# GpSimd clamps exp to [0, 1] by min and max, and VectorE takes over the subtraction, in a fused convolution and ELU network

## The chip, the cores and the metric

The kernel runs on one core of one Trainium2 chip. The metric is the device time of one execution in microseconds (us), as the median of several runs. In the profiles the engines are PE (TensorE; PEld is its weight loads), DVE (VectorE), ACT (ScalarE), POOL (GpSimd) and SP (SyncE, here only an issuer of DMAs; SPq is its queue). "L237" is line 237 of the kernel that was profiled, so a line's number moves a little from one kernel to the next.

## The reference

```python
# x: (8, 4096, 192), weight: (8 heads, 7), w_in: (192, 2048), w_out: (2048, 192), float32
w   = softmax(weight, axis=-1)
out = causal 7-tap convolution of x along the sequence, one filter per head of 24 channels
h   = out.reshape(32768, 192) @ w_in
g   = np.where(h > 0.0, h, 1.0 * (np.exp(np.minimum(h, 0.0)) - 1.0))     # ELU
return g @ w_out
```

The part that matters is ELU on 32768 x 2048 values. Both kernels compute it as max(h, min(exp(h), 1) - 1): for a positive h the right-hand side is 0 and h wins; for a negative h, exp(h) - 1 is at least h and wins.

## The kernel before

The tokens are cut into 32 tiles of 1024. A tile passes 16 "pairs": a pair is 1024 PSUM columns (two halves of 512) of h. Four engines form a line for each pair, each waiting for the one before by semaphores:

1. TensorE: 12 matmuls fill H, one of three PSUM slots.
2. ScalarE: exp of each half into E (4 buffers in SBUF).
3. GpSimd: min with 1 and subtract 1, in place in E, one instruction a half.
4. VectorE: the maximum of E and H into gT, which frees the PSUM slot.

TensorE also does the second matrix product ("ops") of the tile before, and the convolutions of the tile to come.

```python
CONV_AT = (2, 10)     # the steps, of a tile's 16, at which the next tile's two convolutions are issued
# ... (cut)

            # GpSimd
            for n in range(NP):                       # NP = 32 tiles x 16 pairs = 512
                s, i = divmod(n, NQ)
                if i == 8 and s + NXB < NS:
                    load_x(s + NXB)
                for u in range(2):
                    W(s_exp, 2 * n + u + 1)
                    g.tensor_scalar(
                        out=E[:, n % NE, u, :], in0=E[:, n % NE, u, :],
                        scalar1=1.0, scalar2=1.0, op0=ALU.min, op1=ALU.subtract,
                    ).then_inc(s_clp)
# ... (cut)

            # VectorE
            for n in range(NP):
                s, q = divmod(n, NQ)
                W(s_clp, 2 * n + 2)
                if s >= NG3:
                    W(s_mm2, 2 * (s - NG3 + 1))
                v.tensor_tensor(
                    gT[:, s % NG3, 2 * q : 2 * q + 2, :].rearrange("p f t -> p (f t)"),
                    E[:, n % NE, :, :].rearrange("p u t -> p (u t)"),
                    H[:, slot_of_pair[n] % 3, :],
                    ALU.max,
                ).then_inc(s_tt)
# ... (cut)

            # SyncE: once both convolutions of tile s are evacuated to csb, 20 DMAs
            # regroup them into att, which the tile's first H matmul waits for
                    W(s_ce, m + 1)
                    if s >= 2:
                        W(s_h, NQ * (s - 1))
                    for (hb, sl, r0, nr, j, d0) in MOVES:          # 10 moves
                        for r in range(2):
                            sy.dma_start(
                                att[HP * r + d0 : HP * r + d0 + nr, s % 2, j, :, :],
                                csb[SLOT * sl + r0 : SLOT * sl + r0 + nr, s % 2, hb, :, :],
                            ).then_inc(s_att, 16)
```

The 20 "moves" of a tile can start only after its second convolution, which is issued at step 10 of the tile before.

Of the kernel before, what the change touches and what calls it, by code (L numbers as in the profile page):

```python
# [5 lines left out]
ALU = mybir.AluOpType  # L6
# [14 lines left out]
GS = 512  # L21
# [3 lines left out]
NE = 4  # L25
NG3 = 3
# [17 lines left out]
def bass_lightweight_conv__then__act_elu_kernel(  # L44
# [16 lines left out]
    NQ = NF // 2  # L61
# [9 lines left out]
    slot_of_pair, slot_of_conv, prior = {}, {}, []  # L71
# [21 lines left out]
    for n in range(NP + NQ + LAG + NQ):  # L93
        s, i = divmod(n, NQ)
# [10 lines left out]
    with ExitStack() as stack:  # L105
# [16 lines left out]
        E = sbuf("E", [P, NE, 2, GS], FP32)  # L122
        gT = sbuf("gT", [P, NG3, NF, GS], FP16)
# [10 lines left out]
        H = psum("H", [P, 3, 2 * GS])  # L134
# [14 lines left out]
        s_clp = sema("s_clp")  # L149
        s_tt = sema("s_tt")  # L150
# [30 lines left out]
        @block.gpsimd  # L181
        def _gpsimd(g: bass.BassGpSimd):
            W = Waits(g)

            def load_x(s):
                b, t0 = s % NXB, s * SUP
                if s >= NXB:
                    W(s_cv, 2 * (s - NXB) + 2)
                w0 = 0
                if s % SPB == 0:  # L190
                    g.memset(xg[0:6, b, 0, :], 0.0).then_inc(s_z)  # L191
                    g.dma_start(  # L192
                        xg[6:P, b, 0, :], x_flat[t0 : t0 + P - 6, :]
                    ).then_inc(s_x[b], 16)
                    w0 = 1
                src = bass.AP(
                    tensor=x_flat.tensor,
                    offset=(t0 - 6 + CW * w0) * D,
                    ap=[[D, P], [CW * D, 8 - w0], [1, D]],
                )  # L200
                g.dma_start(xg[:, b, w0:8, :], src).then_inc(s_x[b], 16)  # L201
                g.dma_start(  # L202
                    xg[:, b, 8, :], x_flat[t0 + SUP - P : t0 + SUP, :]
                ).then_inc(s_x[b], 16)

            g.memset(shiftm[:], 0.0).then_inc(s_shift)
            load_x(0)
            W(s_shift, 1)
            for d in range(KSIZE):
                g.affine_select(  # L210
                    out=shiftm[:, d, :],
                    in_=shiftm[:, d, :],
                    compare_op=ALU.not_equal,
                    fill=1.0,
                    base=-d,
                    pattern=[[-1, CW]],
                    channel_multiplier=1,
                ).then_inc(s_shift)
            for r in range(2):
                g.dma_start(  # L220
                    w_in[HP * r : HP * (r + 1), :, :],
                    moe_w_in.rearrange("(j p) n -> p j n", p=HP),
                ).then_inc(s_w, 16)
            for r in range(2):
                g.dma_start(  # L225
                    w_out[HP * r : HP * (r + 1), :, :],
                    moe_w_out.rearrange("(f p) d -> p f d", p=HP),
                ).then_inc(s_w, 16)
            for s in range(1, min(NXB, NS)):
                load_x(s)  # L230
# [7 lines that stand above are left out]
                        out=E[:, n % NE, u, :],  # L238
                        in0=E[:, n % NE, u, :],
                        scalar1=1.0,  # L240
                        scalar2=1.0,
                        op0=ALU.min,
                        op1=ALU.subtract,
                    ).then_inc(s_clp)

        @block.scalar
        def _scalar(a):
            W = Waits(a)
            a.memzero(scr[:, 0:1]).then_inc(s_scr)  # L249
            W(s_scr, 1)  # L250
            a.activation(scr[:, 1:2], scr[:, 0:1], ACT.Exp)
            W(s_set, 2)
            a.activation(wex[:], wq2[:], ACT.Exp).then_inc(s_wex)
            n_half = 0

            def evac(n_half):
                W(s_mm2, n_half + 1)
                b = n_half % 2
                W(s_out[b], 32 * (n_half // 2))
                a.activation(  # L260
                    osb[:, b, :, :, :].rearrange("p g k d -> p g (k d)"),
                    ops[:, :, 0 : 2 * D],
                    ACT.Copy,
                ).then_inc(s_oev)

            for item in order:
                if item[0] == "c":
                    m = item[1]
                    s, g = divmod(m, 2)
                    W(s_cv, m + 1)  # L270
                    if s >= 2:
                        W(s_att, 16 * NDMA_ATT * (s - 1))
                    a.activation(  # L273
                        csb[:, s % 2, :, g, :],
                        H[:, slot_of_conv[m] % 3, :].rearrange("p (b t) -> p b t", b=2),
                        ACT.Copy,
                    ).then_inc(s_ce)
                elif item[0] == "h":
                    n = item[1]
                    k = slot_of_pair[n] % 3  # L280
                    W(s_h, n + 1)
                    W(s_tt, n - NE + 1)
                    for u in range(2):
                        a.activation(  # L284
                            E[:, n % NE, u, :], H[:, k, GS * u : GS * (u + 1)], ACT.Exp
                        ).then_inc(s_exp)
                else:
                    _, t, half, r0, r1 = item
                    if r1 == 2 * NF:
                        evac(2 * t + half)  # L290

        @block.vector
        def _vector(v):
            W = Waits(v)
            v.memset(H[:, 0:2, :], 0.0).then_inc(s_hz)  # L295
            W(s_wq, 16)
            v.tensor_reduce(wmx[:], wq[:], AXIS.X, ALU.max).then_inc(s_set)
            W(s_set, 1)
            v.tensor_tensor(
                wq2[:],  # L300
                wq[:],
                wmx[:, :].unsqueeze(2).to_broadcast([P, HEADS, KSIZE]),
                ALU.subtract,
            ).then_inc(s_set)
            W(s_wex, 1)
            v.tensor_reduce(wsum[:], wex[:], AXIS.X, ALU.add).then_inc(s_set)
            W(s_set, 3)
            v.reciprocal(wrs[:], wsum[:]).then_inc(s_set)
            W(s_set, 4)
            v.tensor_tensor(  # L310
                wprb[:],
                wex[:],
                wrs[:, :].unsqueeze(2).to_broadcast([P, HEADS, KSIZE]),
                ALU.mult,
            ).then_inc(s_set)
            v.wait_ge(s_set, 5)
            k = 5
            for d in range(KSIZE):
                W(s_shift, 2 + d)
                sd = shiftm[:, d : d + 1, :].to_broadcast([P, HEADS, CW])  # L320
                wd = wprb[:, :, d : d + 1].to_broadcast([P, HEADS, CW])
                dst = Tm if d == 0 else Ttmp
                v.tensor_tensor(dst[:, :, :], sd, wd, ALU.mult).then_inc(s_set)  # L323
                k += 1
                W(s_set, k)
                if d:
                    v.tensor_tensor(  # L327
                        Tm[:, :, :], Tm[:, :, :], Ttmp[:, :, :], ALU.add
                    ).then_inc(s_set)
                    k += 1  # L330
                    W(s_set, k)
            n_set[0] = k
            for n in range(NP):
                s, q = divmod(n, NQ)
                W(s_clp, 2 * n + 2)
                if s >= NG3:
                    W(s_mm2, 2 * (s - NG3 + 1))
                v.tensor_tensor(  # L338
                    gT[:, s % NG3, 2 * q : 2 * q + 2, :].rearrange("p f t -> p (f t)"),
                    E[:, n % NE, :, :].rearrange("p u t -> p (u t)"),  # L340
                    H[:, slot_of_pair[n] % 3, :],
                    ALU.max,
                ).then_inc(s_tt)

        @block.tensor
        def _tensor(pe):
            W = Waits(pe)

            def wait_slot(k):
                was = prior[k]  # L350
                if was is None:
                    return
                if was[0] == "h":
                    W(s_tt, was[1] + 1)
                else:
                    W(s_ce, was[1] + 1)

            for item in order:
# [45 lines left out]
                else:  # L404
                    _, t, half, r0, r1 = item
                    if r0 == 0:
                        W(s_tt, NQ * (t + 1))
                        W(s_oev, 2 * t + half)
                    for r in range(r0, r1):
                        kb, f = divmod(r, NF)  # L410
# [80 lines left out]
```

## Time and profile before

| | kernel before |
|---|---|
| median time | 2040.86 us (3 runs, 2040.68 to 2042.27) |
| GpSimd busy | 98% of the span |
| chain of waits that ended last | 95% the GpSimd tensor_scalar |
| mean granted TensorE clock | 0.742 of full |

From the profile page of the kernel before. The first line is busy time and share of the span of each engine; the second the granted TensorE clock in 40 slices, in tenths; then the chain that ended last, by engine and by line; then instruction groups: line, engine, operation, output<-input and count, then busy us and mean ns of one, then the idle time of the engine just before them and who ended most of it.

```profile
PE 1057.4 (52%) x25088; PEld 692.6 (34%) x25088; DVE 640.8 (31%) x531; ACT 670.8 (33%) x1156; POOL 1991.8 (98%) x1120
...
PEclk9568777767777766678777677786666787777867
...
POOL 97%; PE 1%; DVE 1%; SPq 1%; DMA 0%; ACT 0%; issue 0%; POOLq 0%
POOL E L237 95%; POOL xg L201 1%; POOL xg L202 1%; SPq L444 1%; PE ops L415 1%; DVE Ttmp L323 0%; DVE Tm L327 0%; POOL xg L192 0%; DMA wq<-in_weight_dram 0%; DMA att<-csb 0%; ACT csb L273 0%; POOLq L105 0%; ACT osb L260 0%; PE H L395 0%; POOL xg L191 0%
...
L237 POOL TENSOR_SCALAR E<-E 128x512 f32<-128x512 f32 x1024 | 1930.5, 1912 | 26.9 <-ACT E L284 26.4
L338 DVE TENSOR_TENSOR gT<-E,H 128x1024 f16<-128x1024 f32 x512 | 625.4, 1221 | 1377.0 <-POOL E L237 1377.0
```

GpSimd is busy for practically the whole span and the chain consists of it. VectorE was idle 1377 us, all of it ended by GpSimd. The other engines have more than 45% of the span to spare.

From the table of waits of the same kernel (us in total, times, longest):

```profile
DVE gT L338 <- POOL E L237: 1377.0, 512, 25.4
...
PE H L395 <- DVE gT L338: 682.7, 407, 2.9
...
PE H L373 <- DVE gT L338: 222.3, 62, 5.4
...
PE H L395 <- DMA att<-csb: 46.6, 14, 17.3
```

TensorE waits for VectorE, which waits for GpSimd; L395 are the matmuls that make h, L373 the convolutions, which need a PSUM slot too. From the chain in order of time, over one tile (start us, us, what):

```profile
1002.02 60.33 POOL E L237 x32
```

Between two DMA issues that GpSimd makes for each tile stand 32 tensor_scalars in a row, 60.33 / 32 = 1.885 us each. A pair takes 2 x 1.885 = 3.77 us. This spacing is a better measure than the group's mean of 1912 ns, in which neighbours overlap a little.

### The profile page before, as it was taken

To read this page: it belongs to the slowest core of one execution; us is meant where nothing else is said; L and a number is where in the kernel's file an instruction comes from. 1 tells how busy PE (TensorE), PEld (TensorE's weight loads), DVE (VectorE), ACT (ScalarE), POOL (GpSimd) and SP (SyncE) were. 2 spreads that over 40 slices of the span, in tenths; PEclk is the share of its full clock that TensorE was granted. 3 is DMA by queue.
4 is the path that set the end of the run, shared out by engine and by line. 5 is a ranking of instruction groups with operands and counts; after the bars stand their busy time and mean duration, and the time that the engine had idled before them with its cause. 6 is when DMAs were issued, how large, how long until landed. Compare 5 with 4: busy or idle time off the path is not lost.

```text
span 2038.9 us, 54519 instructions
## 1 busy us (share of the span) xinstructions
PE 1057.4 (52%) x25088; PEld 692.6 (34%) x25088; DVE 640.8 (31%) x531; ACT 670.8 (33%) x1156; POOL 1991.8 (98%) x1120
## 2 busy tenths in 40 slices
PE   1454544555545556645445555445565554455466
PEld 0132332333323334323333333333333333333344
DVE  3333333333333333333333333333333333333332
ACT  1333333333333333333333333333333333333332
POOL 4999999999999999999999999999999999999996
PEclk9568777767777766678777677786666787777867
DMA  7111022111121210221110221111211102210001
GB/s 104 25 28 31 25 41 41 34 32 32 28 41 33 39 31 22 41 41 33 36 31 25 41 41 34 31 29 32 41 34 37 30 25 41 41 34 27 23 25 33
DMA packets 97717, 71.17 MB, mean 35 GB/s; under 512 B 52048, under 2 KB 84816, under 8 KB 97488
## 3 DMA queue, kind: packets, MB, share of 16 engines
q1 hardware_dynamic: 54928, 50.40, 9.3%
q0 software_dynamic: 42560, 17.29, 7.8%
q8 instruction: 196, 3.21, 0.6%
q14 instruction: 33, 0.27, 0.0%
HBM read 34.59 MB, written 25.17 MB: 29 GB/s over the span
## 4 chain that ended last, share of the span: by engine, by line
POOL 97%; PE 1%; DVE 1%; SPq 1%; DMA 0%; ACT 0%; issue 0%; POOLq 0%
POOL E L237 95%; POOL xg L201 1%; POOL xg L202 1%; SPq L444 1%; PE ops L415 1%; DVE Ttmp L323 0%; DVE Tm L327 0%; POOL xg L192 0%; DMA wq<-in_weight_dram 0%; DMA att<-csb 0%; ACT csb L273 0%; POOLq L105 0%; ACT osb L260 0%; PE H L395 0%; POOL xg L191 0%
## 5 line engine op out<-in xcount | busy, mean ns | idle before, releaser
L237 POOL TENSOR_SCALAR E<-E 128x512 f32<-128x512 f32 x1024 | 1930.5, 1912 | 26.9 <-ACT E L284 26.4
L338 DVE TENSOR_TENSOR gT<-E,H 128x1024 f16<-128x1024 f32 x512 | 625.4, 1221 | 1377.0 <-POOL E L237 1377.0
L395 PE MATMUL H<-att,w_in 64*64 64x512 bf16 x6144 | 556.4, 478 | 729.5 <-DVE gT L338 682.7
L284 ACT ACTIVATE E<-H 128x512 f32<-128x512 f32 x1024 | 555.8, 595 | 1099.4 <-PE H L395 1099.4
L415 PE MATMUL ops<-w_out,gT 64*64 64x192 f16 x16384 | 530.1, 285 | 7.5 <-DVE gT L338 6.1
L415 PEld LDWEIGHTS ops<-w_out,gT 64*64 64x64 f16 x16384 | 476.7, 130 | 138.6 <-issue 77.1
L395 PEld LDWEIGHTS H<-att,w_in 64*64 64x64 bf16 x6144 | 163.1, 123 | 925.5 <-DVE gT L338 753.1
L373 PE MATMUL H<-Tm,xg 128*24 128x122 bf16 (+3 forms) x2560 | 66.3, 284 | 240.4 <-DVE gT L338 222.3
L373 PEld LDWEIGHTS H<-Tm,xg 128*24 128x24 bf16 x2560 | 55.1, 129 | 278.0 <-DVE gT L338 154.2
L273 ACT ACTIVATE csb<-H 128x1024 bf16<-128x1024 f32 x64 | 65.4, 1023 | 234.5 <-PE H L373 234.5
L260 ACT ACTIVATE osb<-ops 128x768 f32<-128x768 f32 x64 | 52.2, 815 | 28.6 <-PE ops L415 28.5
L201 POOL DMA_DIRECT2D xg<-in_x_dram x32 | 31.0, 968 | 0.0
L202 POOL DMA_DIRECT2D xg<-in_x_dram x32 | 18.4, 575 | 0.0
L323 DVE TENSOR_TENSOR Ttmp<-shift,wprb 128x976 bf16<-128x976 bf16 x6 | 7.0, 1175 | 0.2
L192 POOL DMA_DIRECT2D xg<-in_x_dram x8 | 5.0, 626 | 0.0
L327 DVE TENSOR_TENSOR Tm<-Tm,Ttmp 128x976 bf16<-128x976 bf16 x6 | 4.0, 667 | 0.2
L210 POOL TENSOR_SCALAR_AFFINE_SELECT shift<-shift 128x122 bf16<-128x122 bf16 x7 | 2.7, 456 | 0.1
L225 POOL DMA_DIRECT2D w_out<-in_moe_w_out_dram x2 | 2.2, 1102 | 0.0
L295 DVE MEMSET H<- 128x2048 f32 x1 | 1.8, 1765 | 1.3 <-PEq L476 1.3
L191 POOL MEMSET xg<- 6x192 bf16 x8 | 2.0, 247 | 0.0
L249 ACT ACT_TABLE_LOAD x1 | 1.3, 1283 | 0.7 <-PEq L476 0.7
L220 POOL DMA_DIRECT2D w_in<-in_moe_w_in_dram x2 | 1.3, 644 | 0.0
(14 smaller groups left out, 4.5 us busy)
## 6 DMA issues: line engine op xcount, KB each, us to landing
out_dram<-osb SPq DMA_DIRECT2D x128, 192.0 KB, 2.2
att<-csb SPq DMA_DIRECT2D x384, 48.0 KB
xg<-in_x_dram POOLq DMA_DIRECT2D x24, 384.0 KB, 6.4
att<-csb SPq DMA_DIRECT2D x128, 32.0 KB
xg<-in_x_dram POOLq DMA_DIRECT2D x8, 336.0 KB, 5.4
att<-csb SPq DMA_DIRECT2D x128, 16.0 KB
xg<-in_x_dram POOLq DMA_DIRECT2D x32, 48.0 KB, 5.8
w_in<-in_moe_w_in_dram POOLq DMA_DIRECT2D x2, 768.0 KB, 8.1
```

The lines of the kernel that those rows point to most:

```text
L201: g.dma_start(xg[:, b, w0:8, :], src).then_inc(s_x[b], 16)
L202: g.dma_start(xg[:, b, 8, :], x_flat[t0 + SUP - P : t0 + SUP, :]).then_inc(s_x[b], 16)
L237: g.tensor_scalar(out=E[:, n % NE, u, :], in0=E[:, n % NE, u, :], scalar1=1.0, scalar2=1.0, op0=ALU.min, op1=ALU.subtract,).then_inc(s_clp)
L260: a.activation(osb[:, b, :, :, :].rearrange("p g k d -> p g (k d)"), ops[:, :, 0 : 2 * D], ACT.Copy,).then_inc(s_oev)
L273: a.activation(csb[:, s % 2, :, g, :], H[:, slot_of_conv[m] % 3, :].rearrange("p (b t) -> p b t", b=2), ACT.Copy,).then_inc(s_ce)
L284: a.activation(E[:, n % NE, u, :], H[:, k, GS * u : GS * (u + 1)], ACT.Exp).then_inc(s_exp)
L323: v.tensor_tensor(dst[:, :, :], sd, wd, ALU.mult).then_inc(s_set)
L338: v.tensor_tensor(gT[:, s % NG3, 2 * q : 2 * q + 2, :].rearrange("p f t -> p (f t)"), E[:, n % NE, :, :].rearrange("p u t -> p (u t)"), H[ ...
L373: ins = pe.matmul(H[SLOT * q : SLOT * q + CPH, k % 3, GS * hb + o : GS * hb + o + nc_], xg[:, s % NXB, w, CPH * h : CPH * (h + 1)], Tm[:, ...
L395: ins = pe.matmul(H[HP * c : HP * (c + 1), k % 3, GS * r : GS * (r + 1)], w_in[HP * r : HP * (r + 1), j, HP * f : HP * (f + 1)], att[HP * ...
L415: ins = pe.matmul(ops[HP * c : HP * (c + 1), g, D * kb : D * (kb + 1)], gT[HP * g : HP * (g + 1), t % NG3, f, t0 : t0 + HP], w_out[HP * g ...
L444: sy.dma_start(att[HP * r + d0 : HP * r + d0 + nr, s % 2, j, :, :], csb[SLOT * sl + r0 : SLOT * sl + r0 + nr, s % 2, hb, :, :],).then_inc( ...
```

## The change

The intent is to make GpSimd's instruction cheaper. GpSimd keeps one instruction a half, now min with 1 and max with 0. The max changes no value, since exp is never negative. The subtraction goes to VectorE, which does (E - 1) max H in one scalar_tensor_tensor. VectorE's instruction is also cut from 1024 columns to 512, so that it can start after the first half; the semaphore counts double accordingly.

```diff
--- before.py
+++ after.py
@@ -238,9 +238,9 @@
                         out=E[:, n % NE, u, :],
                         in0=E[:, n % NE, u, :],
                         scalar1=1.0,
-                        scalar2=1.0,
+                        scalar2=0.0,
                         op0=ALU.min,
-                        op1=ALU.subtract,
+                        op1=ALU.max,
                     ).then_inc(s_clp)
 
         @block.scalar
@@ -279,7 +279,7 @@
                     n = item[1]
                     k = slot_of_pair[n] % 3
                     W(s_h, n + 1)
-                    W(s_tt, n - NE + 1)
+                    W(s_tt, 2 * (n - NE) + 2)
                     for u in range(2):
                         a.activation(
                             E[:, n % NE, u, :], H[:, k, GS * u : GS * (u + 1)], ACT.Exp
@@ -332,15 +332,18 @@
             n_set[0] = k
             for n in range(NP):
                 s, q = divmod(n, NQ)
-                W(s_clp, 2 * n + 2)
                 if s >= NG3:
                     W(s_mm2, 2 * (s - NG3 + 1))
-                v.tensor_tensor(
-                    gT[:, s % NG3, 2 * q : 2 * q + 2, :].rearrange("p f t -> p (f t)"),
-                    E[:, n % NE, :, :].rearrange("p u t -> p (u t)"),
-                    H[:, slot_of_pair[n] % 3, :],
-                    ALU.max,
-                ).then_inc(s_tt)
+                for u in range(2):
+                    W(s_clp, 2 * n + u + 1)
+                    v.scalar_tensor_tensor(
+                        out=gT[:, s % NG3, 2 * q + u, :],
+                        in0=E[:, n % NE, u, :],
+                        scalar=1.0,
+                        in1=H[:, slot_of_pair[n] % 3, GS * u : GS * (u + 1)],
+                        op0=ALU.subtract,
+                        op1=ALU.max,
+                    ).then_inc(s_tt)
 
         @block.tensor
         def _tensor(pe):
@@ -351,7 +354,7 @@
                 if was is None:
                     return
                 if was[0] == "h":
-                    W(s_tt, was[1] + 1)
+                    W(s_tt, 2 * was[1] + 2)
                 else:
                     W(s_ce, was[1] + 1)
 
@@ -404,7 +407,7 @@
                 else:
                     _, t, half, r0, r1 = item
                     if r0 == 0:
-                        W(s_tt, NQ * (t + 1))
+                        W(s_tt, 2 * NQ * (t + 1))
                         W(s_oev, 2 * t + half)
                     for r in range(r0, r1):
                         kb, f = divmod(r, NF)
```

## The prediction

> **What bounds it now.** GpSimd. The busy table gives POOL 1991.8 us of a 2038.9 us span (98%), PE 52%, ACT 33%, DVE 31%. The chain of waits that ended last is 95% the GpSimd tensor_scalar on E. The instruction groups give 1024 of these at 1912 ns; in the chain, 32 in a row take 60.33 us: 1885 ns each. The table of waits has DVE waiting 1377 us for POOL.
>
> **Removed, added, moved.** POOL keeps 1024 instructions of 128x512 fp32, in place; only the second operation changes, subtract to max. The max with 0 does nothing to the values, since exp is never negative. The subtraction moves into DVE: 512 tensor_tensors over 1024 columns (1221 ns) become 1024 scalar_tensor_tensors over 512. At 1.04 ns per column (estimate from the 0.96 GHz of the Trainium skill, "VectorE: DVE Perf Modes", specifications) 1221 ns leaves 155 ns fixed, so one takes about 690 ns: 1.38 us a pair, about 710 us in all, 80 more than now, off the critical path. ACT and PE work do not change.
>
> **What decides it.** POOL's time per instruction: a nanosecond there is 1.02 us of kernel. From two POOL memsets (192 columns 247 ns, 854 columns 810 ns) I estimate 0.85 ns a column and 84 ns fixed, so a floor near 520 ns for 512 columns. Min+subtract takes 1885 ns, 3.5 ns a column: its software loop holds it, not the port. The Trainium skill, "GPSIMD Engine Reference", section 3.1, has bodies of up to two operations port-bound at 1.03 cycles an element and good loops at 1.8; min+subtract here is far from both (4.2 cycles at its 1.2 GHz). So another pair of operations may take another loop. A max that does nothing makes sense only if min with max is a quick pair. I give that 3 in 4, with 550 to 1000 ns for one. No trace shows it: this is the weak step.
>
> **If quick, the next bound.** POOL: 1024 x 0.55 to 1.0 us + 60 us of its DMA issues = 620 to 1080 us. PE: where it runs back to back (timeline near 1015 us, granted clock 1.0) a pair takes 1.42 us; with convolutions and their waits about 25 us per 16 pairs, so 800 us + 65 us of start and tail. The loop matmul, exp, clamp, max: 0.84 + 1.1 + clamp + 0.69 us plus handovers, some 3.6 us over three PSUM slots, 1.2 us a pair: just below PE. So 860 us (clamp 0.55), 930 (0.8), 1100 (1.0).
> **If not quick:** the kernel stays at 2041 within 1%.
>
> **Prediction.** 950 us, range 790 to 2050 (two-humped: near 950, or near 2041). Faster 0.75, same 0.16, slower 0.09.
>
> **What the profile would show.** Right: POOL group mean at most 1000 ns; POOL share below 95%; DVE's waits for POOL shrink; mean granted PE clock above 0.9 (now 0.74) and PE busy time lower for the same work; DVE group near 690 ns x1024; the chain shared among PE, ACT, DVE. Wrong: POOL group still near 1900 ns and 95% of the chain.
>
> **What would make it wrong.** Max costs POOL as much as subtract (same), or more (slower). DVE and POOL blocking each other on a shared port: not expected, since each DVE instruction reads one operand from SBUF and one from PSUM, and POOL's 1885 ns is steady now whether DVE runs or not. DVE's new form above about 900 ns would become the next bound.

## More of the kernel before

One more line to keep in mind, from the timeline of SyncE's queue: the moves of one tile.

```profile
1009.31 15.03 SPq L444 DMA_DIRECT2D att<-csb  x20
```

Issuing 20 moves takes 15 us. The pairs that are left after step 10 take about 5 x 3.77 = 19 us, so the moves fit behind them.

## The result, and the profile after

| | before | after |
|---|---|---|
| median time | 2040.77 us (4 runs) | 1242.22 us (4 runs, 1241.26 to 1246.92) |
| ratio | 1 | 0.6091 (95% interval 0.6075 to 0.6106) |
| mean granted TensorE clock | 0.742 | 0.863 |

A ratio, here and below, is the mean time of one kernel's fast runs over that of the other's fast runs of the same rounds, so it is not quite the ratio of the medians. All kernels gave correct results.

From the profile page of the changed kernel, the same parts as before:

```profile
PE 818.5 (66%) x25088; PEld 594.9 (48%) x25088; DVE 666.7 (54%) x1043; ACT 656.3 (53%) x1156; POOL 666.4 (54%) x1120
...
PEclk9988889888888887889888898888898888898879
...
SPq 35%; PE 30%; POOL 10%; DVE 8%; ACT 6%; DMA 6%; issue 4%; ACTq 0%; DVEq 0%
SPq L447 35%; PE H L398 16%; PE ops L418 13%; DVE gT L339 7%; POOL E L237 6%; DMA att<-csb 5%; ACT E L284 3%; ACT csb L273 3%; POOL xg L201 2%; PE H L376 2%; POOL xg L202 1%; DVE Ttmp L323 1%; ACT osb L260 0%; DVE Tm L327 0%; POOL xg L192 0%
...
L339 DVE SCALAR_TENSOR_TENSOR gT<-E,H 128x512 f16<-128x512 f32 x1024 | 651.4, 683 | 552.4 <-POOL E L237 533.7
L237 POOL TENSOR_SCALAR E<-E 128x512 f32<-128x512 f32 x1024 | 606.5, 615 | 553.8 <-ACT E L284 552.9
```

GpSimd's mean fell from 1912 to 615 ns and its busy share from 98% to 54%. VectorE's instruction takes 683 ns. But no engine is now near full, and the largest part of the chain, 35%, is SyncE's queue issuing the moves into att. The table of waits says what stands still:

```profile
DVE gT L339 <- POOL E L237: 533.7, 257, 22.1
...
PE H L398 <- DMA att<-csb: 312.7, 32, 17.2
...
PE H L376 <- DVE gT L339: 42.6, 31, 2.1
PE H L398 <- DVE gT L339: 40.1, 78, 0.9
```

TensorE now waits for VectorE only 40.1 us before the matmuls of h (682.7 before the change) and 42.6 us before the convolutions (222.3), but for the moves 312.7 us (46.6 before), 32 times, once a tile. VectorE's 533.7 us for GpSimd are in large part the same standstill passed down the line: GpSimd itself is now idle 553.8 us, and 552.9 us of that ends with ScalarE, as the group's line above says.

One tile, from the timeline of the changed kernel (start us, us for the row, engine, line, operation, count):

```profile
613.01 3.50 POOL L237 TENSOR_SCALAR E<-E 128x512 f32<-128x512 f32 x6
...
615.73 1.02 ACT L273 ACTIVATE csb<-H 128x1024 bf16<-128x1024 f32 x1 [0.47 <-PE H L376]
...
617.72 0.82 PE L398 MATMUL H<-att,w_in 64*64 64x512 bf16 x12
...
619.11 0.82 PE L398 MATMUL H<-att,w_in 64*64 64x512 bf16 x12
```

and, on SyncE's queue in the same stretch:

```profile
616.78 15.81 SPq L447 DMA_DIRECT2D att<-csb  x20
```

The second convolution is evacuated at 616.75 us (ScalarE's row from L273, 615.73 + 1.02). From 616.78 the queue issues 20 moves for 15.8 us. Meanwhile TensorE turns out pairs every 1.39 us (617.72 to 619.11 in the matmul rows) and soon has none left. The six GpSimd instructions at 613.01 stand back to back: 3.50 / 6 = 0.583 us each. What follows the moves:

```profile
633.98 1.50 PE L398 MATMUL H<-att,w_in 64*64 64x512 bf16 x12 [10.53 <-DMA att<-csb]
```

TensorE stood still for 10.53 us until a DMA into att landed. Its 12 matmuls then took 1.50 us where they take 0.82 to 0.84 us otherwise. The clock explains the difference. Busy time of each engine in four stretches, and PEclk, the granted clock (header first):

```profile
core 0: us, PE busy (x) PEld busy (x) DVE busy (x) ACT busy (x) POOL busy (x), PEclk, DMA share, GB/s
624.00:628.00 4.00, 0.00 (x0) 0.00 (x0) 1.28 (x2) 0.00 (x0) 0.63 (x2) 1.00 0.21 51
628.00:634.00 6.00, 0.02 (x4) 0.02 (x4) 0.00 (x0) 0.00 (x0) 0.00 (x0) 0.50 0.21 49
634.00:638.20 4.20, 4.20 (x68) 2.76 (x72) 1.28 (x2) 1.08 (x2) 1.19 (x2) 0.50 0.01 4
638.20:640.00 1.80, 1.80 (x80) 1.29 (x76) 0.44 (x2) 1.75 (x4) 1.07 (x2) 0.99 0.00 0
```

TensorE stopped at about 623.45 us (633.98 - 10.53). The granted clock stayed at 1.00 until 628 us, was 0.50 for the rest of the standstill and for 4.2 us of work after it, and was full again from 638.2 us. The Trainium skill, "TensorE: Matmul & The Clock Gate", Part 1, says that the array falls to half clock when it idles and that about 3.4 us of sustained work brings it back. This trace agrees in kind; in this tile the fall came about 4.5 us after the stop, and the return after 4.2 us of work.

### The profile page after: what moved, and what is told of

It reads as the page before. It is cut to its first block, busy times and chain, and to the rows that moved or that the text cites. A ratio compares the mean times of both kernels' runs of the same rounds, so it can differ in the third digit from the quotient of the medians.

```text
span 1240.6 us, 55031 instructions
## 1 busy us (share of the span) xinstructions
PE 818.5 (66%) x25088; PEld 594.9 (48%) x25088; DVE 666.7 (54%) x1043; ACT 656.3 (53%) x1156; POOL 666.4 (54%) x1120
## 4 chain that ended last, share of the span: by engine, by line
SPq 35%; PE 30%; POOL 10%; DVE 8%; ACT 6%; DMA 6%; issue 4%; ACTq 0%; DVEq 0%
SPq L447 35%; PE H L398 16%; PE ops L418 13%; DVE gT L339 7%; POOL E L237 6%; DMA att<-csb 5%; ACT E L284 3%; ACT csb L273 3%; POOL xg L201 2%; PE H L376 2%; POOL xg L202 1%; DVE Ttmp L323 1%; ACT osb L260 0%; DVE Tm L327 0%; POOL xg L192 0%
## 5 line engine op out<-in xcount | busy, mean ns | idle before, releaser
L339 DVE SCALAR_TENSOR_TENSOR gT<-E,H 128x512 f16<-128x512 f32 x1024 | 651.4, 683 | 552.4 <-POOL E L237 533.7
L237 POOL TENSOR_SCALAR E<-E 128x512 f32<-128x512 f32 x1024 | 606.5, 615 | 553.8 <-ACT E L284 552.9
L398 PE MATMUL H<-att,w_in 64*64 64x512 bf16 x6144 | 470.2, 414 | 353.5 <-DMA att<-csb 312.7
L418 PEld LDWEIGHTS ops<-w_out,gT 64*64 64x64 f16 x16384 | 406.4, 115 | 107.4 <-issue 33.8
L418 PE MATMUL ops<-w_out,gT 64*64 64x192 f16 x16384 | 452.3, 256 | 4.0 <-issue 2.1
L398 PEld LDWEIGHTS H<-att,w_in 64*64 64x64 bf16 x6144 | 169.5, 115 | 445.2 <-DMA att<-csb 302.4
L273 ACT ACTIVATE csb<-H 128x1024 bf16<-128x1024 f32 x64 | 66.5, 1040 | 35.7 <-PE H L376 35.7
L376 PE MATMUL H<-Tm,xg 128*24 128x122 bf16 (+3 forms) x2560 | 41.6, 211 | 60.7 <-DVE gT L339 42.6
L376 PEld LDWEIGHTS H<-Tm,xg 128*24 128x24 bf16 x2560 | 32.9, 93 | 88.9 <-DVE gT L339 56.6
```

What stands on the lines that cost most here:

```text
L237: g.tensor_scalar(out=E[:, n % NE, u, :], in0=E[:, n % NE, u, :], scalar1=1.0, scalar2=0.0, op0=ALU.min, op1=ALU.max,).then_inc(s_clp)
L273: a.activation(csb[:, s % 2, :, g, :], H[:, slot_of_conv[m] % 3, :].rearrange("p (b t) -> p b t", b=2), ACT.Copy,).then_inc(s_ce)
L339: v.scalar_tensor_tensor(out=gT[:, s % NG3, 2 * q + u, :], in0=E[:, n % NE, u, :], scalar=1.0, in1=H[:, slot_of_pair[n] % 3, GS * u : GS * ...
L376: ins = pe.matmul(H[SLOT * q : SLOT * q + CPH, k % 3, GS * hb + o : GS * hb + o + nc_], xg[:, s % NXB, w, CPH * h : CPH * (h + 1)], Tm[:, ...
L398: ins = pe.matmul(H[HP * c : HP * (c + 1), k % 3, GS * r : GS * (r + 1)], w_in[HP * r : HP * (r + 1), j, HP * f : HP * (f + 1)], att[HP * ...
L418: ins = pe.matmul(ops[HP * c : HP * (c + 1), g, D * kb : D * (kb + 1)], gT[HP * g : HP * (g + 1), t % NG3, f, t0 : t0 + HP], w_out[HP * g ...
```

## The experiments

Theory A: the gain is GpSimd's shorter instruction, which comes from the pair of operations. Rivals: the finer split of VectorE's work (B), or the departure of the subtraction as such (E below). Theory C: what still separates 1242 us from the predicted 950 us is the wait for the moves, which GpSimd's slowness used to cover. Rival D: the loop through the PSUM slots limits anyway. Ten kernels ran, in three sessions, each on a chip of its own with shared runs of the kernel before: experiments 1, 2, 7 and 8 first (median of before 2041.60 us), then 3 and 4 (2042.98 us), then 5, 6, 9 and 10 (2042.35 us). All kernels but one ran in 3 rounds with a profiled run besides, 4 runs in all.

### 1. Only the split (split_only)

```diff
 # kernel before; GpSimd keeps min and subtract; the semaphore counts double as in the change (cut)
-                W(s_clp, 2 * n + 2)
-                v.tensor_tensor(gT[... 1024 columns], E[... 1024], H[... 1024], ALU.max).then_inc(s_tt)
+                for u in range(2):
+                    W(s_clp, 2 * n + u + 1)
+                    v.tensor_tensor(gT[... 512 columns], E[... 512], H[... 512], ALU.max).then_inc(s_tt)
```

> The kernel before, with min and subtract on GpSimd, and only VectorE's maximum split into two tensor_tensors of 512 columns. Theory A: 2041 us within 0.5%, GpSimd 1912 ns and 98% busy. Rival B: visibly faster, under 1950 us.

Measured: 2041.62 us, ratio 0.9999 (0.9984 to 1.0014). GpSimd's mean in its profile is 1911 ns. The split alone is worth nothing while GpSimd is the bound.

### 2. The change without the split (unsplit)

```diff
 # changed kernel; the semaphore counts go back to those of before (cut)
-                for u in range(2):
-                    W(s_clp, 2 * n + u + 1)
-                    v.scalar_tensor_tensor(out=gT[... 512 columns], ...).then_inc(s_tt)
+                W(s_clp, 2 * n + 2)
+                v.scalar_tensor_tensor(out=gT[... 1024 columns], ...).then_inc(s_tt)
```

> The changed kernel, but VectorE does one scalar_tensor_tensor over 1024 columns per pair, as the kernel before did with its maximum. Theory A (the whole gain is GpSimd's time per instruction, 1885 to about 590 ns): GpSimd stays near 615 ns in the profile and the time stays within 3% of 1242 us, so 1220 to 1280. Rival B (the split into 512 columns carries a good part of the gain, by shortening the loop through the three PSUM slots): above 1350 us. VectorE's instruction should be near 1221 ns.

Measured: 1269.87 us, ratio to before 0.6217 (0.6207 to 0.6226), against 0.6091 with the split. The group of VectorE, from its page:

```profile
L338 DVE SCALAR_TENSOR_TENSOR gT<-E,H 128x1024 f16<-128x1024 f32 x512 | 620.1, 1221 | 613.2 <-POOL E L237 612.8
```

So the new operations alone bring 2042 to 1270 us; the split adds some 28 us, 2%. Rival B falls. The two-operation form costs VectorE nothing over the one-operation maximum: 1221 ns for 1024 columns in both kernels.

### 3. Min alone (min_alone)

```diff
 # changed kernel
-                        scalar1=1.0, scalar2=0.0, op0=ALU.min, op1=ALU.max,
+                        scalar1=1.0, scalar2=None, op0=ALU.min,
```

> The changed kernel without the maximum with 0: GpSimd does min with 1 alone, one operation. The result is the same. Theory E (a loop without the subtraction is quick): GpSimd at or below 615 ns and the time within 2% of 1242 us. Rival F (only the pair of min and max has the quick loop, which is why a maximum that changes no value was put in): GpSimd well above 900 ns and a time well above 1300 us.

Measured: 1642.95 us, ratio 0.8039 (0.8026 to 0.8053). From its page, the GpSimd group:

```profile
L237 POOL TENSOR_SCALAR E<-E 128x512 f32<-128x512 f32 x1024 | 1490.0, 1485 | 73.7 <-ACT E L283 68.9
```

Taking away an operation that changes no value makes GpSimd's instruction 2.4 times as long (615 to 1485 ns) and the kernel 400 us slower. Theory E falls: less arithmetic is not what makes it quick.

### 4. Eleven choices of operations, by themselves (op_pairs)

```diff
 # changed kernel, after GpSimd's main loop; pin and pout are tiles of their own
+            for r in range(6):
+                W(s_pr, 0 + r)
+                g.tensor_scalar(out=pout[:, 0 : (512 if r % 2 else 128)], in0=pin[:, 0 : (512 if r % 2 else 128)],
+                                scalar1=1.0, scalar2=0.5, op0=ALU.min, op1=ALU.max).then_inc(s_pr)
+            # ... (cut) the same for ten more choices of op0, op1, each on a line of its own
```

> The changed kernel with a row of GpSimd tensor_scalars after its main loop, on a tile of their own, nothing else using GpSimd: each of eleven choices of operations on 128 and on 512 columns of float32, three times each, each waiting for the one before. Theory E (subtract is what costs): min+max, max+min, min+min and min alone about 590 ns at 512 columns; every form with subtract, and perhaps with add or mult, about 1885 ns, subtract alone in between. Rival F (only min+max, in this order, is quick): all others 1400 ns and more. Rival G (the mix of a comparison with an arithmetic operation costs): mult+add, add+add and all single operations quick as well, and only min+subtract, subtract+min and subtract+max slow.

From the instruction groups of that run, shapes kept apart, POOL only; each is one choice, three instructions, mean ns behind the busy us. The lines are L253 min, max; L256 max, min; L259 min, min; L262 min, subtract; L265 subtract, min; L268 subtract, max; L271 mult, add; L274 add, add; L277 min alone; L280 subtract alone; L283 mult alone.

```profile
L274 POOL TENSOR_SCALAR pout<-pin 128x512 f32<-128x512 f32 x3 | 5.8, 1922 | 0.2
L262 POOL TENSOR_SCALAR pout<-pin 128x512 f32<-128x512 f32 x3 | 5.8, 1919 | 0.2
L265 POOL TENSOR_SCALAR pout<-pin 128x512 f32<-128x512 f32 x3 | 5.8, 1919 | 0.2
L268 POOL TENSOR_SCALAR pout<-pin 128x512 f32<-128x512 f32 x3 | 5.8, 1919 | 0.2
L259 POOL TENSOR_SCALAR pout<-pin 128x512 f32<-128x512 f32 x3 | 5.7, 1915 | 0.2
L256 POOL TENSOR_SCALAR pout<-pin 128x512 f32<-128x512 f32 x3 | 5.7, 1914 | 0.3
...
L283 POOL TENSOR_SCALAR pout<-pin 128x512 f32<-128x512 f32 x3 | 4.5, 1490 | 0.2
L280 POOL TENSOR_SCALAR pout<-pin 128x512 f32<-128x512 f32 x3 | 4.5, 1489 | 0.2
L277 POOL TENSOR_SCALAR pout<-pin 128x512 f32<-128x512 f32 x3 | 4.5, 1484 | 0.2
...
L262 POOL TENSOR_SCALAR pout<-pin 128x128 f32<-128x128 f32 x3 | 1.9, 640 | 0.2
...
L271 POOL TENSOR_SCALAR pout<-pin 128x512 f32<-128x512 f32 x3 | 1.9, 621 | 0.2
L253 POOL TENSOR_SCALAR pout<-pin 128x512 f32<-128x512 f32 x3 | 1.8, 614 | 0.2
...
L277 POOL TENSOR_SCALAR pout<-pin 128x128 f32<-128x128 f32 x3 | 1.6, 529 | 0.2
...
L253 POOL TENSOR_SCALAR pout<-pin 128x128 f32<-128x128 f32 x3 | 0.9, 294 | 0.2
```

Three classes appear, and nothing lies between them:

| choice | ns at 512 columns | ns a column, from 128 to 512 |
|---|---|---|
| min, max; mult, add | 614; 621 | (614 - 294) / 384 = 0.83 |
| any one operation alone | 1484 to 1490 | (1484 - 529) / 384 = 2.49 |
| every other pair, max, min among them | 1914 to 1922 | (1919 - 640) / 384 = 3.33 |

No theory got all of it. Theory E is wrong again, since min, min holds no subtraction and is slow. Rival G is wrong, since add, add and the single operations are slow. Rival F is nearly right: min, max is quick and its reverse is not; but mult, add is quick as well. What the pair does inside GpSimd no trace shows; shown is only that two ordered pairs of the eight tried are three times as fast as the rest. The number for min, max is the same after the main loop, where VectorE has nothing left to do but for the first microsecond (614 ns), as in the main loop beside VectorE (615 ns), so in this kernel VectorE does not hold GpSimd up.

### 5. The same two operations in the other order (max_min)

```diff
 # changed kernel
-                        scalar1=1.0, scalar2=0.0, op0=ALU.min, op1=ALU.max,
+                        scalar1=0.0, scalar2=1.0, op0=ALU.max, op1=ALU.min,
```

> The changed kernel with the same two operations of GpSimd in the other order: first the maximum with 0, then the minimum with 1. Same arithmetic, same count of instructions, same work everywhere else. If the quick loop belongs to the ordered pair min, max (as the row of pairs showed: 614 ns against 1914 ns), GpSimd is at about 1912 ns and the time back at 2041 us within 1%: all of the gain gone. If order does not matter in the main loop: 1242 us within 1%.

Measured: 2036.86 us, ratio 0.9972 (0.9955 to 0.9988). From its page:

```profile
L237 POOL TENSOR_SCALAR E<-E 128x512 f32<-128x512 f32 x1024 | 1926.9, 1909 | 26.8 <-ACT E L284 26.4
```

All of the gain but 0.3% is gone, with the same arithmetic, instructions and semaphores. This is the cleanest evidence for the cause of the gain.

### 6. The subtraction back on GpSimd, in the other quick pair (mult_add)

```diff
 # changed kernel
-                        scalar1=1.0, scalar2=0.0, op0=ALU.min, op1=ALU.max,          # GpSimd
+                        scalar1=1.0, scalar2=-1.0, op0=ALU.mult, op1=ALU.add,
-                        scalar=1.0, ... op0=ALU.subtract, op1=ALU.max,               # VectorE
+                        scalar=0.0, ... op0=ALU.min, op1=ALU.max,
```

> The changed kernel with the subtraction back on GpSimd, as mult by 1 and add of -1, and the clamp on VectorE: minimum with 0, then maximum with h, in the same scalar_tensor_tensor. The result is the same. If what counts is that the pair is one of the two quick ones: GpSimd near 621 ns, VectorE near 683 ns, 1242 us within 1%. If it counts that the subtraction left GpSimd: GpSimd near 1900 ns and about 2041 us.

Measured: 1241.85 us, ratio 0.6080 (0.6064 to 0.6096), no different from the change. From its page:

```profile
L237 POOL TENSOR_SCALAR E<-E 128x512 f32<-128x512 f32 x1024 | 614.4, 622 | 547.7 <-ACT E L284 546.8
```

GpSimd subtracts here, and the kernel is as fast. It is the pair that counts, not where the subtraction is done. Five of the eleven choices have now run in the main loop too, in place and with other constants, and took what the row of experiment 4 has for them, within 1%: min, subtract 1912 ns; min, max 615; min alone 1485; max, min 1909; mult, add 622.

### 7. The moves started earlier (early_conv)

```diff
 # changed kernel
-CONV_AT = (2, 10)
+CONV_AT = (0, 2)
```

> The changed kernel with the next tile's two convolutions issued at steps 0 and 2 of 16 instead of 2 and 10, so that the 20 moves into att (15 us to issue and 2 us to land) start 8 pairs earlier. Theory C (of the 1241 us, the wait of TensorE for the moves into att, 313 us, is exposed time and nothing else stands behind it): the wait falls below 40 us and the time to 930 to 980 us. Rival D (the loop of matmul, exp, clamp and maximum through three PSUM slots, or the engines' handovers, limits anyway): the wait for the moves goes, but waits of TensorE for VectorE grow, and the time stays above 1100 us.

Measured: 870.08 us (868.58 to 872.22), ratio to before 0.4259 (0.4252 to 0.4266). From its page, the engines, the clock and the chain by engine:

```profile
PE 750.8 (86%) x25088; PEld 552.3 (63%) x25088; DVE 663.7 (76%) x1043; ACT 651.7 (75%) x1156; POOL 667.4 (77%) x1120
...
PEclk9999999999999999999999999999999999999999
...
PE 51%; POOL 12%; SPq 11%; DVE 10%; ACT 7%; issue 6%; DMA 3%; ACTq 0%; DVEq 0%
```

and from its waits of TensorE:

```profile
PE H L398 <- DVE gT L339: 68.9, 74, 2.1
PE H L398 <- DMA att<-csb: 21.6, 6, 17.2
...
PE H L376 <- DVE gT L339: 0.4, 1, 0.4
```

The wait for the moves fell from 312.7 to 21.6 us, 17.2 us of it at the start. TensorE's wait for VectorE rose from 40.1 to 68.9 us before the matmuls of h but fell from 42.6 to 0.4 us before the convolutions, so in all it fell a little, from 82.7 to 69.3 us, and rival D falls. Theory C's mechanism holds, but its size was too small: 870 us against the expected 930 to 980. The spans tell why. They fell by 1240.6 - 870.3 = 370.3 us. TensorE's busy time fell by 818.5 - 750.8 = 67.7 us for the same instructions, since its clock is at 0.991 now; its idle time fell by the other 302.6 us. The wait for the moves is 291.1 us of the idle time. The expectation had counted this wait and left out the cold clock after each one, and the convolutions' waits. This version beats both kernels.

### 8. The same edit on the kernel before (before_early_conv)

```diff
 # kernel before
-CONV_AT = (2, 10)
+CONV_AT = (0, 2)
```

> The kernel before, with the same early convolutions at steps 0 and 2. Theory C (with GpSimd at 3.77 us a pair, the five pairs after step 10 take 19 us, which covers the 17 us of the moves): no change, 2041 us within 0.5%. If the moves had cost the kernel before time as well, it would be faster.

Measured: 2042.26 us, ratio 1.0002 (0.9987 to 1.0017). The edit that is worth 370 us after the change is worth nothing before it. The place of the convolutions was a good choice for a kernel with 3.77 us a pair.

### 9. Half way (conv_mid)

```diff
 # changed kernel
-CONV_AT = (2, 10)
+CONV_AT = (2, 6)
```

> The changed kernel with the second convolution at step 6 of 16, half way between the change (10) and the early version (2). If the exposed wait is just the 17 us of the moves less the work that is left in the tile, four pairs more cover 4 x 1.42 us = 5.7 us of about 9.5 us a tile: the wait for the moves falls from 313 us to about 140 us and the time to 1040 to 1085 us. If it is all or nothing (a stall of another kind that the early version happens to avoid): near 1242 us or near 870 us.

Measured: 1043.01 us (1037.89 to 1047.89), ratio 0.5106 (0.5083 to 0.5130). From its waits of TensorE:

```profile
PE H L398 <- DMA att<-csb: 141.8, 32, 17.2
```

The wait fell by 312.7 - 141.8 = 170.9 us, over 31 tiles 5.5 us each, for four pairs of 1.39 us (5.6 us). It is a remainder, the length of the moves less the work left to cover them, and not all or nothing. The mean clock rose to 0.936 on the way.

### 10. Early convolutions without the split (early_unsplit)

The edits of experiments 2 and 7 together.

> The early convolutions together with VectorE's one instruction of 1024 columns per pair. In the changed kernel the split was worth 2%. If the split pays only where TensorE waits for the loop and not for the moves, it should pay as much or more here, where the wait for the moves is gone: 885 to 930 us against 870 us, and TensorE's wait for VectorE above the 69 us of the split version.

Measured: 914.86 us (911.61 to 916.25), ratio 0.4477 (0.4468 to 0.4486), against 0.4259 with the split. From its waits of TensorE:

```profile
PE H L397 <- DVE gT L338: 115.9, 108, 2.6
```

The split is worth 45 us here (5%), 28 us in the change (2%) and nothing before it. TensorE's wait for VectorE before the matmuls of h is 115.9 us without it and 68.9 us with it, 47 us less, which is about what the split is worth here. So the split pays most where the greater waits, for GpSimd and for the moves, are gone.

## Why the prediction was right or wrong

- **What bounds the kernel before, and what a nanosecond of GpSimd is worth:** right. Experiment 5 puts GpSimd's instruction back to 1909 ns with everything else as changed, and the time returns to 2037 us.
- **The weak step, that min with max is a quick pair:** right. It was inferred from a max that does nothing; no trace of before showed it. It was not foreseen that their order matters. The estimated floor of 520 ns at 512 columns was near: 583 ns back to back, and 0.83 ns a column against the 0.85 estimated. The range given was 550 to 1000 ns.
- **VectorE at about 690 ns:** right, 683 ns; with the 1221 ns of experiment 2 for 1024 columns, that is (1221 - 683) / 512 = 1.05 ns a column, against the 1.04 of the estimate. **DVE and GpSimd not blocking each other:** right, 614 ns after the loop and 615 ns in it.
- **The next bound:** this is the step that failed on size. The prediction's sum had "with convolutions and their waits about 25 us per 16 pairs, so 800 us + 65 us of start and tail", which for a clamp of 0.55 to 0.8 us gave 860 to 930 us. The term of the convolutions' waits was mis-sized. In the changed kernel the H matmuls run from 37.3 to 1218.8 us, (1218.8 - 37.3) / 32 = 36.9 us a tile. What was left out is the moves: 15 us to issue and 2 us to land, starting at step 10. They were invisible in the shares of before, because five slow pairs covered them. With pairs at 1.39 us about 9.5 us of them shows in every tile ((312.7 - 17.2) / 31), and the clock is cold after it: the 67.7 us that TensorE is busy longer than in experiment 7 are another 2.1 us a tile. Experiment 7 takes the moves off the path and has 25.4 us a tile ((849.1 - 37.3) / 32), the 25 us of the sum.
- **Granted clock above 0.9:** wrong, 0.863, for the same reason; 0.991 once the wait is gone.
- **The loop of 1.2 us a pair just below TensorE:** consistent with experiment 7, where TensorE waits for VectorE 68.9 us of 870. **The chain shared among PE, ACT and DVE:** wrong in the change (SyncE's queue leads with 35%), and only partly so in experiment 7 (PE 51%, POOL 12%, SPq 11%, DVE 10%, ACT 7%).
- The central 950 us stood for the quick case and was 292 us too low; the measured time lies above even the 1100 us that the sum gave for the slowest clamp of that case. The range held it only because it reached up to the 2041 us of the other case, which is luck.

Open: why these two ordered pairs are quick, and whether other pairs, types or shapes are; only eleven choices in float32 were tried. What is left of TensorE's idle time in the early version (it is busy 86% of the span) was not pursued.

## What to carry to other kernels

The time of GpSimd's tensor_scalar in float32 could not be told from the count of its operations. Measure the pairs by themselves in one run before designing around them: here a useless second operation bought a factor of 2.4, and swapping two operations cost a factor of 3. When the bound is lifted, go through every wait that is short in the old profile and ask what covers it. A transfer that needs 17 us behind five slow pairs needs about twelve quick ones (an estimate: 17 / 1.39), and the place where it starts has to move along with the change.

## What the Trainium skill lacked or had wrong

- "GPSIMD Engine Reference", section 3.1, has bodies of up to two operations at 1.03 cycles an element. At its 1.2 GHz the pairs min, max and mult, add agree (0.83 ns a column, 1.0 cycle). A single operation does not (2.49 ns, 3.0 cycles), nor do six other pairs (3.33 ns, 4.0 cycles). The choice of operations decides here, and the page has no list of quick ones.
- The same page, section 4.1, calls one-input work on GpSimd "roughly line-rate". For tensor_scalar in float32 that holds, of the eleven choices tried, only for those two pairs: 614 and 621 ns for 512 columns, against 1484 to 1922 ns.
- No page says that the order counts. "FP8 and Floating Point Precision", section "FP32 → FP8 Conversion", gives the clamp as min, then max, also on GpSimd, without a word on its speed. That order took 614 ns, the reverse 1914 ns.
- "DMA: Bandwidth & Descriptors", section "Issuing engines are not separate DMA queues", calls the time to initiate a DMA usually small relative to the DMA itself. Here 20 moves of 16 to 48 KB took 15 to 16 us to issue from one queue (0.71 us at the median), and the last one landed about 2.1 us after its issue began. A single issue is about a third of that, but 20 in a row on one queue were most of the 17 us from the first issue to the last landing.
